# Attention phase of a fused attention and expert kernel: one hand-written order of six entries per block, queries and keys laid out by block

## Chip, cores and metric

One core of one Trainium2 chip. The metric is the device time of one execution in microseconds (us); the kernel before takes 626.17 us (median of 3 runs, 625.88 to 626.33).

## What is computed

Windowed attention over 2 batches, 8 heads, 576 positions and 64 columns a head; its output, 1152 tokens of 512 columns, goes through a dense mixture of 4 experts and then through a two-layer network. Everything is float32.

```python
scores = scale * np.matmul(q, k.transpose(0, 1, 3, 2))
mask = (rel >= 0) & (rel < 64)                    # rel = query position - key position
attn = softmax(np.where(mask, scores, -1e9))
x = attn @ v                                      # heads side by side: 1152 x 512
x = sum_e p[:, e] * (relu(x @ w1[e]) @ w2[e])     # 4 experts, 512 -> 1024 -> 512
h = x @ w_in                                      # 512 -> 2048
return (max(h, 0) + alpha * min(h, 0)) @ w_out    # 2048 -> 512
```

## The kernel before

Queries are taken in 18 blocks of 64 rows (9 to a batch); a block needs its own 64 keys and the 64 before it. Four pairs of heads are worked side by side, so that a block is 128 partitions (two heads of 64 queries) by 4 pairs by 128 keys. Every block j goes through these steps, each a function that issues instructions to several engines:

- **S** (`att_S`, L302): TensorE multiplies queries and keys (L309, 8 products, 16 records in the trace) into two PSUM banks; in the same function VectorE adds the mask and takes the row extreme, once for each pair (L320).
- **E** (`att_E`, L324): ScalarE takes the exponential with its row sum, once for each pair (L327).
- **N** (`att_N`, L330): VectorE adds 1e-9 and inverts the sums (L332, L333), GpSimd scales the block (L334).
- **PT** (`att_PT`, L336): TensorE transposes the four pairs (L340); ScalarE copies them out of PSUM (L346), or VectorE does (L344) for odd j from 4 on.
- **PV** (`att_PV`, L349): TensorE multiplies by the values (L357). The result is the token block x in three forms: raw (`xr`), a rounded high part and a low part. For the last block of a chunk ScalarE makes the high part (L365) and VectorE the low part (L366) and the copy (L367); else VectorE copies (L369) and GpSimd makes high and low (L370, L371). PV also loads the values of block j + 6.

The tokens are then taken in four chunks (256, 256, 256, 384). For the first slice of 512 expert columns, `l1_chunk` (called LC; **L c f**, L500) multiplies a chunk by 128 columns of w1 in 12 products of 256 columns, in the order w1-low by x-high, w1-high by x-low, w1-high by x-high; `l2_chunk` (BC; **B c t**, L533) multiplies by w2. The weights are split into high and low parts first: **W f** (`split_w1`, L228 ScalarE, L230 GpSimd for even f and VectorE for odd f) and **V f** (`split_w2`, L219 ScalarE, L212 VectorE). **X** (`x_second`) prepares sums for later slices, **R** (`p_prep`) the expert shares. After the fourth chunk come the other slices, over 500 us of products.

Order. The whole program runs under `manual_schedule`: an engine works through its instructions in the order in which the functions are called. That order is made by a loop over j that appends steps to a list (L603 on), and by marks: L 0 0 comes after PV 3 and four further steps, and after each L and B the list is advanced in proportion. The start is, as called:

```
S_0 E_0 S_1 E_1 N_0 S_2 E_2 N_1 W_0 PT_0 S_3 E_3 N_2 W_1 Q_3 PT_1 N_3 S_4 E_4 PV_0 W_2 PT_2 N_4
S_5 E_5 PV_1 W_3 PT_3 N_5 S_6 PV_2 Q_4 PV_3 E_6 PT_4 S_7 N_6 L_0_0 V_0 R L_0_1 V_1 E_7 PT_5 S_8 ...
```

The V splits are planned into L 0 0 to L 0 3. PSUM is eight banks taken in turn; S takes two, the others one.

Loads. All DMAs are issued by SyncE (SP) in program order: queries of a group of three blocks (`load_q`, L117, 384 KB; **Q g** later), keys (`load_k`, L120; first three blocks 384 KB, then the other six, 768 KB; batch 1 whole with Q 3), values (`load_v`, L129, L131), weight slices of 1 MB (`load_w`, L144, two buffers). A slice's load is placed after the last use of the slice two before it.

Of the kernel before, what the change touches and what calls it, by code (L numbers as in the profile page):

```python
# [8 lines left out]
F32 = mybir.dt.float32  # L9
# [7 lines left out]
P = 128  # L17
# [9 lines left out]
def tile_kernel(ctx, tc, q, k, v, probs, w1, w2, w_in, w_out, alpha, out):  # L27
    nc = tc.nc


    B, H, D, S = k.shape
    NP = H // 2
# [3 lines left out]
    BLK = 64  # L36
# [58 lines left out]
    for c in range(1, NCH):  # L95
        n = CHUNK[c + 1] - CHUNK[c]
        xc.append([w0.tile([P, KD, 384], F32R, tag=f"xc{w}", bufs=2, name=f"xc{w}{c}")[:, :, 0:n] for w in "hl"])
    kts = [ab.tile([P, NP, BLK + S], F32, name=f"kt{i}") for i in range(B)]

    qs = [ab.tile([P, NP, GRP], F32, name=f"q{i}") for i in range(3)]  # L100

# [12 lines left out]

    def load_q(g):
        b, i = divmod(g, S // GRP)
        nc.sync.dma_start(out=qs[g % 3], in_=q[b, i])  # L117

    def load_k(b, t0, t1):
        nc.sync.dma_start(out=kts[b][:, :, BLK + t0:BLK + t1],  # L120
                          in_=k[b].rearrange("(a h) d t -> (h d) a t", h=2)[:, :, t0:t1])

# [102 lines left out]
    def split_w1(f):  # L225
        hv, lv = [x.rearrange("p (k m) -> p k m", k=KD) for x in w_tiles(1, 0, f)]
        src = ws_t[1, 0][:, :, f * P:(f + 1) * P]
        nc.scalar.activation(out=hv, in_=src, func=AF.Copy)  # L228
        e = nc.vector if f % 2 else nc.gpsimd
        e.tensor_tensor(out=lv, in0=src, in1=hv.bitcast(F32), op=ALU.subtract)  # L230
# [65 lines left out]

    v_t, ws_t, wd_t, w_t, wf_t, h_t, p_t, pt_t = {}, {}, {}, {}, {}, {}, {}, {}

    def att_S(j):
        g, jb = divmod(j, GB)  # L300
        m = mask0 if j % NB == 0 else mask

        ps = [psum(f"s{j}_{i}")[:, 0:NP // 2 * P].rearrange("p (a k) -> p a k", k=P) for i in range(2)]
        sv = [ps[hp % 2][:, hp // 2, :] for hp in range(NP)]

        for hp in range(NP):
            for h in range(2):
# [40 lines left out]

    def att_PV(j):  # L349
# [230 lines left out]

    with tc.manual_schedule():
        load_q(0)
        load_k(0, 0, GRP)
        nc.vector.memset(kts[0][:, :, 0:BLK], 0.0)
        make_mask(mask0, True)
        load_v(0)
        load_v(1)
        make_identity(nc, ident)
        make_mask(mask, False)
        nc.gpsimd.memset(kts[1][:, :, 0:BLK], 0.0)  # L590
        load_k(0, GRP, S)
# [10 lines left out]

        NG = NBLK // GB  # L603
        steps = []
        for j in range(NBLK + 4):
            last = (j - 3) * BLK in CHUNK[1:]
            pv = [("PV", j - 4)] if 0 <= j - 4 < NBLK else []

            if last:
                steps += pv  # L610
            apart = 6 <= j - 1 < 14
            if apart:
                steps.append(("E", j - 1))
            if j == NBLK:
                steps.append(("N", j - 1))
            if 0 <= j - 3 < NBLK:
                steps.append(("PT", j - 3))
            if 3 < j < NBLK and not apart:
                steps.append(("N", j - 1))
            if j < NBLK:  # L620
                steps.append(("S", j))
                if not 6 <= j < 14:
                    steps.append(("E", j))
            if 0 < j <= 3:
                steps.append(("N", j - 1))
            if not last:
                steps += pv
            if apart:
                steps.append(("N", j - 1))
            if 2 <= j < 2 + NF:  # L630
                steps.append(("W", j - 2))
            if j % GB == 0 and 3 <= j // GB + 2 < NG:
                steps.append(("Q", j // GB + 2))

            if 12 <= j < 17:
                steps.append(("X", j - 12))
        pos = [0]

        def att_step():
            op, j = steps[pos[0]]  # L640
            pos[0] += 1
            if op == "Q":
                load_q(j)
                if j == 3:
                    load_k(1, 0, S)
            elif op == "S":
                att_S(j)
            elif op == "E":
                att_E(j)
            elif op == "N":  # L650
                att_N(j)
            elif op == "W":
                split_w1(j)
            elif op == "X":
# [23 lines left out]
        def LC(c):  # L678
            return [("LC", c, f) for f in range(NF)]
# [101 lines left out]

        marks = [steps.index(("PV", CHUNK[c + 1] // BLK - 1)) + 1 for c in range(NCH)]
        per = [len(LC(c) + BC(c)) for c in range(NCH)]
        while pos[0] < marks[0] + 4:
            att_step()
        for tid in loads.get(-1, ()):
# [9 lines left out]
        for i, unit in enumerate(order):  # L796
            op = unit[0]
            if op == "END":
                while pos[0] < len(steps):
                    att_step()  # L800
                at_cm.__exit__(None, None, None)
# [37 lines left out]
            if op in ("LC", "BC") and unit[1] < NCH - 1:  # L839
                c = unit[1]  # L840
                n = (unit[2] if op == "LC" else NF + unit[2]) + 1
                while pos[0] < min(len(steps), marks[c] + (marks[c + 1] - marks[c]) * n // (per[c] - 1)):
                    att_step()

# [38 lines left out]
```

## Time and profile before

| | |
|---|---|
| median of 3 runs | 626.17 us |
| profiled execution, its own time | 626.92 us |
| its span, first to last instruction | 624.9 us |
| PE busy | 610.9 us (98%) |
| ScalarE (ACT) busy | 316.6 us (51%) |
| VectorE (DVE) busy | 468.9 us (75%) |
| GpSimd (POOL) busy | 280.7 us (45%) |
| mean granted TensorE clock | 0.995 |

The sum of a change is made against the span. What lies around the span is 626.92 - 624.9 = 2.0 us. PE is TensorE's products, PEld its weight loads. A timeline row gives the start, the duration, engine, line, operation, what is written from what, and in brackets how long the engine sat idle before it and what released it.

### The profile page before, as it was taken

The page shows a single profiled execution, that of the slowest core. Times are in us where ns is not written, and L with a number is a line of the kernel's source. Part 1 is how long each engine was busy: PE and PEld are TensorE (multiplying, and loading weights), DVE is VectorE, ACT ScalarE, POOL GpSimd, SP SyncE. Part 2 cuts the span into 40 slices and gives each one's busy share as a digit, 9 for nine tenths or more (in the row PEclk, how much of TensorE's full clock was granted, in tenths as well). Part 3 has the DMA queues.
Part 4 walks back from the last instruction along what each step waited for, and adds up shares of the span by engine and source line. Part 5 has one row for each costly group of instructions (what it writes and reads, how often), then busy time and mean ns, then how long its engine had stood idle before and what let it go on. Part 6 is the DMA issues. An engine that isn't in the chain of part 4 may idle for free.

```text
span 624.9 us, 10887 instructions
## 1 busy us (share of the span) xinstructions
PE 610.9 (98%) x4032; PEld 549.2 (88%) x4032; DVE 468.9 (75%) x937; ACT 316.6 (51%) x789; POOL 280.7 (45%) x297
## 2 busy tenths in 40 slices
PE   4899999999999999999999999999999999999998
PEld 3688899989989989989989989988898988988986
DVE  3776659779888779878878879746978879764642
ACT  5656536634633724634633724635777753651730
POOL 5646661145153443445253443603735677661440
PEclk9799999999999999999999999999999999999999
DMA  9842002415414514415314514003401412310012
GB/s 320 314 160 65 6 1 65 139 34 177 161 51 144 160 35 151 153 59 180 135 50 141 164 34 131 39 7 120 145 1 36 157 79 69 105 64 1 2 50 102
DMA packets 31653, 62.60 MB, mean 100 GB/s; under 512 B 2288, under 2 KB 11760, under 8 KB 30576
## 3 DMA queue, kind: packets, MB, share of 16 engines
q1 hardware_dynamic: 31600, 61.90, 29.4%
q8 instruction: 32, 0.52, 0.3%
q14 instruction: 21, 0.17, 0.1%
HBM read 51.14 MB, written 10.75 MB: 99 GB/s over the span
## 4 chain that ended last, share of the span: by engine, by line
PE 96%; DMA 1%; ACT 1%; DVE 1%; SPq 0%; issue 0%
PE o L545 43%; PE X L431 23%; PE Z L431 11%; PE W L431 6%; PE h L500 5%; PE oc L533 4%; PE pv L357 1%; DMA ws<-in_moe_w_dram 1%; PE pt L340 1%; PE s L309 1%; ACT p L327 1%; PE x L578 1%; ACT w1h L228 0%; ACT ptr L346 0%; SPq L117 0%
## 5 line engine op out<-in xcount | busy, mean ns | idle before, releaser
L545 PE MATMUL o<-w2l,hh 128*128 128x512 f32 (+1 forms) x400 | 155.5, 389 | 0.0
L545 PE MATMUL o<-w2h,hl 128*128 128x512 f32 (+1 forms) x400 | 155.3, 388 | 0.0
L545 PE MATMUL o<-w2h,hh 128*128 128x512 f32 (+1 forms) x400 | 154.9, 387 | 0.0
L292 POOL TENSOR_TENSOR ct<-ct 128x512 f32<-128x512 f32 x32 | 44.0, 1374 | 118.8 <-DVE ct L291 53.3
L545 PEld LDWEIGHTS o<-w2h,hl 128*128 128x128 f32 x400 | 75.1, 188 | 16.5 <-POOL hl L526 1.2
L545 PEld LDWEIGHTS o<-w2h,hh 128*128 128x128 f32 x400 | 75.1, 188 | 14.8
L545 PEld LDWEIGHTS o<-w2l,hh 128*128 128x128 f32 x400 | 75.1, 188 | 14.5
L564 DVE SCALAR_TENSOR_TENSOR acc<-o,pn,acc 128x512 f32<-128x512 f32 x63 | 47.1, 748 | 38.8 <-PE o L545 38.6
L187 POOL TENSOR_TENSOR sr<-ws 128x256 f32<-128x256 f32 x44 | 40.7, 926 | 72.4 <-DVE wfl L212 61.5
L212 DVE SCALAR_TENSOR_TENSOR w2l<-ws,w2h 128x512 fp32r<-128x512 f32 x48 | 42.7, 896 | 20.8 <-ACT w2h L219 20.5
L431 PE MATMUL X<-xth,wfl 128*128 128x256 f32 (+1 forms) x264 | 56.7, 296 | 0.0
L431 PE MATMUL X<-xtl,wfh 128*128 128x256 f32 (+1 forms) x264 | 56.6, 295 | 0.0
L431 PE MATMUL X<-xth,wfh 128*128 128x256 f32 (+1 forms) x264 | 56.6, 295 | 0.0
L219 ACT ACTIVATE wfh<-sr 128x1024 fp32r<-128x1024 f32 x22 | 23.2, 1058 | 53.5 <-POOL sr L187 53.5
L293 POOL TENSOR_TENSOR ct<-ct 128x512 f32<-128x512 f32 x32 | 47.3, 1478 | 2.5
L280 ACT ACTIVATE ct<-wd 128x512 f32<-128x512 f32 x32 | 21.3, 667 | 47.4 <-DVE ct L286 47.4
L568 DVE TENSOR_TENSOR acc<-o,acc 128x512 f32<-128x512 f32 (+1 forms) x28 | 18.8, 670 | 33.2 <-PE o L545 33.1
L431 PEld LDWEIGHTS X<-xtl,wfh 128*128 128x128 f32 x264 | 42.7, 190 | 0.0
L431 PEld LDWEIGHTS X<-xth,wfl 128*128 128x128 f32 x264 | 42.7, 190 | 0.0
L431 PEld LDWEIGHTS X<-xth,wfh 128*128 128x128 f32 x264 | 42.6, 190 | 0.0
L526 POOL TENSOR_TENSOR hl<-s,hh 128x256 fp32r<-128x256 f32 (+1 forms) x16 | 13.3, 852 | 61.2 <-ACT hh L525 61.2
L431 PE MATMUL Z<-xth,wfl 128*128 128x320 f32 (+1 forms) x176 | 37.9, 296 | 0.0
(155 smaller groups left out, 1425.9 us busy)
## 6 DMA issues: line engine op xcount, KB each, us to landing
ws<-in_moe_w_dram SPq DMA_DIRECT2D x16, 1024.0 KB, 5.6
wd<-in_moe_w_in_dram SPq DMA_DIRECT2D x16, 512.0 KB, 3.8
cv<-ct SPq DMA_DIRECT2D x32, 256.0 KB, 2.7
wd<-in_moe_w_out_dram SPq DMA_DIRECT2D x16, 512.0 KB, 3.6
ws<-cv SPq DMA_DIRECT2D x8, 1024.0 KB, 5.3
v<-in_v_dram SPq DMA_DIRECT2D x16, 256.0 KB, 5.2
q<-in_q_dram SPq DMA_DIRECT2D x6, 384.0 KB, 6.6
out_dram<-acc SPq DMA_DIRECT2D x8, 256.0 KB, 2.0
```

What stands on the lines that cost most here:

```text
L187: e.tensor_tensor(out=t4[:, o], in0=x, in1=y, op=op)
L212: nc.vector.scalar_tensor_tensor(out=lv, in0=src, scalar=1.0, in1=hv.bitcast(F32), op0=ALU.mult, op1=ALU.subtract)
L219: nc.scalar.activation(out=hv, in_=src, func=AF.Copy)
L280: nc.scalar.activation(out=a, in_=top.bitcast(F32), func=AF.Abs, scale=LIFT)
L292: nc.gpsimd.tensor_tensor(out=y, in0=y, in1=e, op=ALU.mult)
L293: nc.gpsimd.tensor_tensor(out=y, in0=r, in1=y, op=ALU.add)
L431: nc.tensor.matmul(ps, lhsT=w[:, d, :], rhs=x[:, d, :], start=(first and m == 0), stop=(m == 5), skip_group_check=True)
L500: nc.tensor.matmul(ps, lhsT=w[:, d * P:(d + 1) * P], rhs=x[:, d, :], start=(m == 0), stop=(m == 3 * KD - 1))
L533: nc.tensor.matmul(ps, lhsT=h_c[c, f][a][:, t * P:(t + 1) * P], rhs=w_t[2, 0, f][b], start=(n == 0), stop=(n == 3 * NF - 1))
L545: nc.tensor.matmul(ps, lhsT=h_t[s, p, f][a][:, t * P:(t + 1) * P], rhs=w_t[2, s, f][b][:, cols], start=(n == 0), stop=(n == 3 * NF - 1))
L564: nc.vector.scalar_tensor_tensor(out=at, in0=ps, scalar=sc, in1=at, op0=ALU.mult, op1=ALU.add)
L568: nc.vector.tensor_tensor(out=at, in0=ps, in1=at, op=ALU.add)
```

## The change

- `att_S` is cut in two: **S** keeps the products, the masking becomes **M** (`att_M`). Blocks have six entries: S, M, E, N, PT, PV.
- The loop and the marks go. One table names every step of the attention phase, with W, V, R, Q, X and the places of L and B.
- Queries lie in DRAM and SBUF as (block, pair, 64), keys too, with one empty block in front. The products take the keys of two neighbouring blocks as two pieces of 64. The first block of queries and of keys is loaded by DMAs of its own (128 KB each), the other two blocks of the group after them. The later keys of both batches come in two parts; the order of the first loads is another.
- PT 0 and PT 1 are copied by VectorE. PV 2 is handled like the last block of a chunk. W's low part goes to VectorE for even f, to GpSimd for odd f.
- The load of w1's next slice stands after L 0 0 in program order, ahead of W 3.

```diff
-    kts = [ab.tile([P, NP, BLK + S], F32, name=f"kt{i}") for i in range(B)]
-    qs = [ab.tile([P, NP, GRP], F32, name=f"q{i}") for i in range(3)]
+    kts = [ab.tile([P, NB + 1, NP, BLK], F32, name=f"kt{i}") for i in range(B)]
+    qs = [ab.tile([P, GB, NP, BLK], F32, name=f"q{i}") for i in range(3)]
...
+    def load_q(g, a=0, z=GB):
         b, i = divmod(g, S // GRP)
-        nc.sync.dma_start(out=qs[g % 3], in_=q[b, i])
+        nc.sync.dma_start(out=qs[g % 3][:, a:z], in_=q[b, i, :, a:z])
+    def load_k(b, a, z):
+        nc.sync.dma_start(out=kts[b][:, 1 + a:1 + z], in_=k[b, :, a:z])
...
-        e = nc.vector if f % 2 else nc.gpsimd
+        e = nc.gpsimd if f % 2 else nc.vector
...
                 nc.tensor.matmul(
-                    sv[hp][c],
-                    lhsT=qs[g % 3][r, hp, jb * BLK:(jb + 1) * BLK],
-                    rhs=kts[j // NB][r, hp, (j % NB) * BLK:(j % NB) * BLK + P],
+                    sv[hp][c].rearrange("p (n t) -> p n t", n=2),
+                    lhsT=qs[g % 3][r, jb, hp, :],
+                    rhs=kts[j // NB][r, j % NB:j % NB + 2, hp, :],
...
+        m_t[j] = sv, m
+    def att_M(j):
+        sv, m = m_t.pop(j)
...
-        if j % 2 and j >= NF:
+        if j in (0, 1) or j % 2 and j >= NF:
             nc.vector.tensor_copy(out=t, in_=src)
...
-        if (j + 1) * BLK in CHUNK:
+        if j == 2 or (j + 1) * BLK in CHUNK:
...
+        load_q(0, 0, 1)
+        load_k(0, 0, 1)
+        nc.vector.memset(kts[0][:, 0], 0.0)
         make_mask(mask0, True)
+        load_q(0, 1, GB)
+        load_k(0, 1, GB)
         load_v(0)
...
         load_q(1)
+        load_k(0, GB, 2 * GB)
+        load_v(1)
         load_w((1, 0))
         load_v(2)
         load_v(3)
+        load_k(0, 2 * GB, NB)
+        load_q(2)
         load_w((2, 0))
         load_v(4)
         load_v(5)
...
-                if j == 3:
-                    load_k(1, 0, S)
+                if j in (3, 4):
+                    load_k(1, *((0, GB) if j == 3 else (GB, NB)))
...
+        TABLE = (
+            "S_0 S_1 M_0 M_1 E_0 N_0 S_2 M_2 S_3 Q_3 E_1 N_1 M_3 PT_0 E_2 N_2 E_3 S_4 M_4 N_3 PT_1 S_5 PV_0 "
+            "E_4 M_5 PT_2 PV_1 N_4 W_0 PT_3 PV_2 W_1 PV_3 S_6 Q_4 W_2 E_5 M_6 N_5 S_7 L_0_0 V_0 W_3 E_6 M_7 "
+            "S_8 N_6 M_8 V_1 L_0_1 PT_4 L_0_2 V_2 L_0_3 V_3 E_7 PT_5 PV_4 N_7 E_8 S_9 Q_5 S_10 PT_6 M_9 R_0 "
+            "N_8 B_0_0 E_9 M_10 PV_5 E_10 PV_6 PT_7 B_0_1 PV_7 PT_8 S_11 N_9 M_11 L_1_0 N_10 E_11 L_1_1 PT_9 "
...
+            "M_16 L_2_2 E_16 PV_12 X_4 PT_14 N_16 S_17 L_2_3 M_17 E_17 PV_13 N_17 PT_15 B_2_0 PV_14 PT_16 "
+            "PV_15 PT_17 PV_16 PV_17 B_2_1")
...
-        tids = [(1, 0)] + tids
-        uses[1, 0] = [-1]
+        tids = [(1, 0), (2, 0)] + tids
+        uses[1, 0], uses[2, 0] = [last_use["W"]], [last_use["V"]]
```

## Rows read from the trace of the kernel before

**Rows 1.** Busy time by stretch: us, then PE, PEld, DVE, ACT, POOL (instructions), granted clock, DMA share, GB/s

```profile
5.73:14.87 9.14, 7.05 (x89) 5.33 (x89) 5.07 (x38) 7.14 (x33) 3.46 (x4) 1.00 1.05 385
14.87:22.35 7.48, 4.52 (x92) 3.35 (x88) 4.75 (x24) 6.54 (x24) 6.19 (x8) 0.96 1.06 384
22.35:25.52 3.17, 3.17 (x37) 2.39 (x37) 2.86 (x14) 2.00 (x10) 2.62 (x4) 0.50 1.06 373
25.52:29.85 4.33, 4.33 (x29) 4.33 (x26) 2.08 (x14) 1.31 (x3) 1.83 (x3) 0.64 0.80 262
...
29.85:84.16 54.31, 54.14 (x630) 45.44 (x629) 36.44 (x153) 29.78 (x116) 32.36 (x41) 1.00 0.21 67
84.16:624.90 540.74, 537.67 (x3169) 488.33 (x3167) 417.40 (x695) 268.56 (x604) 230.64 (x224) 1.00 0.27 91
```

**Rows 2.** The same view for one pair of first-layer units, L 1 0 and L 1 1

```profile
45.53:48.51 2.98, 2.98 (x28) 2.98 (x25) 1.62 (x11) 0.55 (x2) 1.04 (x1) 1.00 0.05 14
```

**Rows 3.** Timeline of TensorE

```profile
5.73 2.83 PE L309 MATMUL s<-kt,q 64*64 64x128 f32 x48 [5.73 <-DMA kt<-in_k_dram]
10.65 1.11 PE L340 MATMUL pt<-ident,p 128*128 128x128 f32 x4 [2.09 <-POOL p L334]
...
13.81 1.13 PE L309 MATMUL s<-kt,q 64*64 64x128 f32 x16
14.87 0.71 PE L357 MATMUL pv<-ptr,v 128*64 128x64 f32 x16
...
16.44 0.67 PE L309 MATMUL s<-kt,q 64*64 64x128 f32 x16
...
22.35 1.12 PE L357 MATMUL pv<-ptr,v 128*64 128x64 f32 x16 [2.03 <-ACT ptr L346]
...
25.52 1.22 PE L500 MATMUL h<-xah,w1l 128*128 128x256 f32 x4
```

**Rows 4.** Timeline of ScalarE

```profile
7.34 0.40 ACT L327 ACTIVATE p<-sm,st 128x128 f32<-128x128 f32 x1 [5.33 <-DVE st L320]
...
8.90 0.39 ACT L327 ACTIVATE p<-sm,st 128x128 f32<-128x128 f32 x1
...
21.21 0.61 ACT L228 ACTIVATE w1h<-ws 128x512 fp32r<-128x512 f32 x1
21.73 0.57 ACT L346 ACTIVATE ptr<-pt 128x512 f32<-128x512 f32 x1
...
23.52 0.39 ACT L365 ACTIVATE xah<-pv 128x256 fp32r<-128x256 f32 x1 [1.22 <-PE pv L357]
```

**Rows 5.** Timeline of VectorE, the first two masking instructions of block 0

```profile
7.01 0.29 DVE L320 CUSTOM_DVE_ANT_0 sm<-s,mask 128x128 f32<-128x128 f32 x1 [5.88 <-PE s L309]
...
7.22 0.29 DVE L320 CUSTOM_DVE_ANT_0 sm<-s,mask 128x128 f32<-128x128 f32 x1
```

**Rows 6.** Groups of instructions, 0 to 25.5 us: count, busy us, mean ns, idle before

```profile
L334 POOL TENSOR_TENSOR p<-p,st 128x512 f32<-128x512 f32 x6 | 6.2, 1038 | 7.0 <-DVE st L333 6.6 <-PE pv L357 0.4
L332 DVE TENSOR_SCALAR st<-st 128x4 f32<-128x4 f32 x6 | 2.5, 417 | 1.3 <-ACT p L327 1.3
L230 POOL TENSOR_TENSOR w1l<-ws,w1h 128x512 fp32r<-128x512 f32 x2 | 2.5, 1270 | 1.1 <-ACT w1h L228 1.0
L230 DVE TENSOR_TENSOR w1l<-ws,w1h 128x512 fp32r<-128x512 f32 x2 | 1.4, 692 | 2.0 <-ACT w1h L228 2.0
```

**Rows 7.** First two windows of 5 us, last two columns DMA share and GB/s

```profile
0.00:5.00 5.00, 0.00 (x0) 0.00 (x0) 0.27 (x1) 1.28 (x1) 3.63 (x17) 1.00 0.63 197
5.00:10.00 5.00, 2.83 (x48) 2.46 (x48) 2.72 (x25) 2.66 (x14) 0.44 (x1) 1.00 1.05 369
...
```

**Rows 8.** DMA issue to landing, first query transfer, first key transfer, first weight slice

```profile
q<-in_q_dram SPq DMA_DIRECT2D x1, 384.0 KB, 3.0
...
kt<-in_k_dram SPq DMA_DIRECT2D x1, 384.0 KB, 4.4
...
ws<-in_moe_w_dram SPq DMA_DIRECT2D x1, 1024.0 KB, 8.6
```

More of the change, by code (lines that the diff above doesn't have):

```diff
@@ L28, in tile_kernel @@
     nc = tc.nc
-    B, H, D, S = k.shape
+    B, S, H, D = v.shape
     NP = H // 2
@@ L112, in make_mask @@
             nc.gpsimd.memset(m[:, 0:BLK], NEG)
-    def load_q(g):
+    def load_q(g, a=0, z=GB):
         b, i = divmod(g, S // GRP)
-        nc.sync.dma_start(out=qs[g % 3], in_=q[b, i])
-    def load_k(b, t0, t1):
-        nc.sync.dma_start(out=kts[b][:, :, BLK + t0:BLK + t1],
-                          in_=k[b].rearrange("(a h) d t -> (h d) a t", h=2)[:, :, t0:t1])
+        nc.sync.dma_start(out=qs[g % 3][:, a:z], in_=q[b, i, :, a:z])
+    def load_k(b, a, z):
+        nc.sync.dma_start(out=kts[b][:, 1 + a:1 + z], in_=k[b, :, a:z])
     def load_v(j):
@@ L295, in conv_steps @@
         store()
-    v_t, ws_t, wd_t, w_t, wf_t, h_t, p_t, pt_t = {}, {}, {}, {}, {}, {}, {}, {}
+    v_t, ws_t, wd_t, w_t, wf_t, h_t, m_t, p_t, pt_t = {}, {}, {}, {}, {}, {}, {}, {}, {}
     def att_S(j):
@@ L581, in tile_kernel @@
     with tc.manual_schedule():
-        load_q(0)
-        load_k(0, 0, GRP)
-        nc.vector.memset(kts[0][:, :, 0:BLK], 0.0)
+        load_q(0, 0, 1)
+        load_k(0, 0, 1)
+        nc.vector.memset(kts[0][:, 0], 0.0)
         make_mask(mask0, True)
+        load_q(0, 1, GB)
+        load_k(0, 1, GB)
         load_v(0)
-        load_v(1)
         make_identity(nc, ident)
         make_mask(mask, False)
-        nc.gpsimd.memset(kts[1][:, :, 0:BLK], 0.0)
-        load_k(0, GRP, S)
+        nc.gpsimd.memset(kts[1][:, 0], 0.0)
         load_q(1)
+        load_k(0, GB, 2 * GB)
+        load_v(1)
         load_w((1, 0))
@@ L595, in tile_kernel @@
         load_v(3)
+        load_k(0, 2 * GB, NB)
+        load_q(2)
         load_w((2, 0))
-        load_q(2)
         load_v(4)
@@ L601, in tile_kernel, with att_step @@
         nc.sync.dma_start(out=alph, in_=alpha)
[L603 to L641, printed above, removed]
+        def att_step(op, j):
             if op == "Q":
                 load_q(j)
-                if j == 3:
-                    load_k(1, 0, S)
+                if j in (3, 4):
+                    load_k(1, *((0, GB) if j == 3 else (GB, NB)))
             elif op == "S":
                 att_S(j)
+            elif op == "M":
+                att_M(j)
             elif op == "E":
@@ L653, in att_step @@
                 split_w1(j)
+            elif op == "V":
+                split_w2(0, j)
+            elif op == "R":
+                p_prep()
             elif op == "X":
@@ L682, in BC @@
             return [("BC", c, t) for t in range((CHUNK[c + 1] - CHUNK[c]) // P)]
-        order = LC(0) + BC(0) + LC(1) + BC(1) + LC(2) + BC(2) + [("END",)]
-        order += LC(3) + [("X1",)] + BC(3)
+        TABLE = (
[8 rows of a table added]
+        order, steps, last_use = [], [[]], {}
+        for word in TABLE.split():
+            op, *j = word.split("_")
+            j = [int(x) for x in j]
+            if op in ("L", "B"):
+                order.append((op + "C", *j))
+                steps.append([])
+            else:
+                steps[-1].append((op, *j))
+                last_use[op] = len(order) - 1
+        order += [("END",)] + LC(3) + [("X1",)] + BC(3)
         for s in range(1, S1):
@@ L698, in plan @@
             work.setdefault(at[unit], []).append((fn, tid, args))
-        for f in range(NF):
-            plan(("LC", 0, f), split_w2, (2, 0), 0, f)
         for s in range(1, NST):
@@ L780, in tile_kernel @@
                 loads.setdefault(free, []).append(tid)
[L782 to L785, printed above, removed]
+        for step in steps[0]:
+            att_step(*step)
         for tid in loads.get(-1, ()):
@@ L798, in tile_kernel @@
             if op == "END":
-                while pos[0] < len(steps):
-                    att_step()
                 at_cm.__exit__(None, None, None)
@@ L814, in tile_kernel @@
             elif op == "LC":
-                while pos[0] < marks[unit[1]]:
-                    att_step()
                 l1_chunk(*unit[1:])
@@ L824, in tile_kernel @@
                     pend.append((i + 2, unit[2], unit[3]))
-            if i == 0:
-                p_prep()
             while pend and pend[0][0] <= i:
@@ L839, in tile_kernel @@
             if op in ("LC", "BC") and unit[1] < NCH - 1:
[L840 to L843, printed above, removed]
+                for step in steps[i + 1]:
+                    att_step(*step)
 _INS = ['q', 'k', 'v', 'moe_domain_probs', 'moe_w1', 'moe_w2', 'moe2_w_in', 'moe2_w_out', 'moe2_alpha']
@@ L862 @@
             b, h, s, d = a.shape
-            a = _np.ascontiguousarray(a.reshape(b, h // 2, 2, s // 192, 192, d).transpose(0, 3, 2, 5, 1, 4).reshape(b, s // 192, 2 * d, h // 2, 192))
+            a = a.reshape(b, h // 2, 2, s // 192, 3, 64, d).transpose(0, 3, 2, 6, 4, 1, 5)
+            a = _np.ascontiguousarray(a.reshape(b, s // 192, 2 * d, 3, h // 2, 64))
         elif name == "k":
-            a = _np.ascontiguousarray(a.transpose(0, 1, 3, 2))
+            b, h, s, d = a.shape
+            a = a.reshape(b, h // 2, 2, s // 64, 64, d).transpose(0, 2, 5, 3, 1, 4)
+            a = _np.ascontiguousarray(a.reshape(b, 2 * d, s // 64, h // 2, 64))
         elif name == "v":
```

2 rows, old and new, of the table TABLE are left out of this document.

## The prediction, made before the change was run

> **What bounds the kernel now.** I read the busy table by stretch first [rows 1]. From 29.85 us on TensorE is busy 54.14 of 54.31 us and then 537.67 of 540.74, so nothing that moves work among the other engines is worth anything there; the reader should see that the loss lies ahead of 29.85. It has three parts. Until 5.73 us TensorE waits for keys [rows 3]. From 5.73 to 22.35 it works 7.05 + 4.52 of 16.6 us. From 22.35 to about 28.6 it works without pause at the 1.2 GHz level (granted clock 0.50, then 0.64 on the mean of the next 4.33 us) [rows 1].
>
> The timelines say why. TensorE comes to PV 3 at 22.35 after 2.03 us of waiting for ScalarE's copy of PT 3 [rows 3]; on ScalarE that copy starts at 21.73, right behind W 3 at 21.21 [rows 4]. ScalarE is busy 7.14 of 9.14 us, then 6.54 of 7.48 [rows 1]: it is the bound there, and in its order stand things that the first L does not need yet. Up to that copy it does six E (1.56 us each, from 7.34 to 8.90 [rows 4]), four W and four copies (0.52 and about 0.55 each [rows 4]): 9.4 + 2.1 + 2.2 = 13.7 of the 15 us since 7.34. L 0 0 starts at 25.52 [rows 3].
>
> The clock needs a word. The record says 1.00 from the start, but an S takes 1.13 us at 13.81 and 0.67 at 16.44, and PV at 14.87 is the first fast step [rows 3]; I go by the durations: 1.2 GHz until 14.87, 2.4 until about 21.8, 1.2 again after the wait of 2.03 us. A step (S, PT, PV) costs some 1.05 us at the low level and 0.6 at the high one, from start to start.
>
> **The change, part by part.** I walk the new order from the first landing to L 0 0; all times below are estimates put together from the rows named.
>
> First landing. Before, 384 KB of queries landed at 0.73 + 3.0 = 3.7 us and the keys at 1.17 + 4.4 = 5.57 [rows 8]. Now S 0 needs 256 KB in two transfers. Bounds: 3.2 (128 KB less than the queries) and 5.57 (no gain); I take 3.7, the nearest row. S 1 and S 2 need the same 768 KB as before: 5.5. The second group ends with byte 1.70 MB: 0.985 MB are moved by 5.0 us (197 GB/s), the rest at 369 GB/s takes 1.95 [rows 7], and some 0.95 passes to landing: S 3 at 8.0. W1's slice comes 0.39 MB earlier in the queue than before, where it landed at 3.87 + 8.6 = 12.4 [rows 8], so at about 11.4; ScalarE asks for it at 15.5. Two more DMA issues cost SP about 0.45 us each, hidden since the engines are full until 25 us [rows 1]. The 384 KB of later keys and queries that now stand ahead of w2 put it at about 17.5; V 0 asks at 20.
>
> Masks and exponentials. M starts 1.28 us after its S (5.73 to 7.01) and takes 4 x 0.21 = 0.85 [rows 5]; E starts 0.33 after M [rows 4, 5]. N takes 0.42 + 0.18 on VectorE and 1.04 on GpSimd [rows 6]. So M 0 5.0, E 0 5.3 to 6.9, M 1 6.8 to 7.65, E 1 7.1 to 8.7, N 0 7.65 to 8.25, GpSimd 8.35 to 9.4. M 2 8.25, E 2 8.7 to 10.25, M 3 9.7 (behind N 1), E 3 10.25 to 11.8.
>
> TensorE, low clock: PT 0 9.4, S 4 10.45, PT 1 11.5, S 5 12.55, PV 0 13.6. VectorE copies PT 0 at 10.55 to 11.2 (0.69, like its W part [rows 6]), N 2 to 11.8, M 4 to 12.65, N 3 to 13.25, copy of PT 1 to 13.95. E 4 12.15 to 13.7. TensorE is then dense from 9.4 on. Before, the first step at the high level was a PV that ended a dense run of PT and S [rows 3]; so I take the high level from PV 0 on. PV 0 ends 14.3, PT 2 14.9, PV 1 15.5, PT 3 16.1.
>
> ScalarE: copy of PT 2 14.95 to 15.5, W 0 to 16.05, copy of PT 3 16.1 to 16.65, high part of PV 2 16.85 to 17.2 (0.39 [rows 4]), W 1 to 17.75, high part of PV 3 to 18.1. VectorE: raw copy of PV 0 to 14.7, M 5 to 15.55, copy of PV 1 to 16.0, N 4 to 16.6, W 0's low part (0.69) to 17.3, PV 2's to 18.1, PV 3's low part to 18.55. GpSimd holds W 1's low part (1.27 [rows 6]) until about 19.5; L 0 1 asks at 20.8. TensorE: PV 2 16.1, PV 3 16.8, S 6 and S 7 17.45 to 18.65. **L 0 0 starts at about 18.6**; its low x parts are asked 0.47 later.
>
> Sum. L 0 0 comes 25.52 - 18.6 = 6.9 us earlier. It and L 0 1 run at the high clock: before they took 4.33 us [rows 1], another pair takes 2.98 [rows 2], 1.35 gained. PT 4 stood ahead of L 0 0 and now stands behind: 0.6 back. Gain 6.9 + 1.35 - 0.6 = 7.7 us. Bounds: if ScalarE had no gap from 5.3 on, five E, two copies, two W and two high parts take 7.8 + 1.1 + 1.1 + 0.7 = 10.7 and L 0 0 starts at 16.1, a gain of 10.2. Below, the rivals.
>
> A rule on the clock. The row shows TensorE rising to the high level at 14.87 out of a run in which PT and S took turns [rows 3]. The Trainium skill, TensorE: Matmul & The Clock Gate, Part 4: PE-mode transpose, says that transposes do not bring up the full clock, as they don't count as busy like other products. By that rule the new stretch, with its four PT, would stay low, and the gain would be 2.9 instead of 7.7. The sum goes by the row.
>
> Moves that cost nothing, and their cover. E 5, W 2, W 3 and R go behind or close to L 0 0: ScalarE's 3.1 us and VectorE's share then run beside four L (6 us) and S 8 to S 10; in the stretch after, ScalarE was busy 29.78 and VectorE 36.44 of 54.31 [rows 1]. W 3's low part on GpSimd ends at about 23, L 0 3 asks at 24.5; without that 1.5 us TensorE would stand. The load of w1's next slice now waits on SP for W 3's low part; behind it stand values of blocks 10 and up, first read 20 us later. M 9 on VectorE waits behind N 7, which waits for E 7 until 28.6; PT 7 asks for N 7 near 33. The thinnest cover is at L 1 0: between PV 7 and it stand now only PT 8 and S 11 (1.2 us), for a high part of 0.39 and a low one of 0.4; before, B 0 1 (3 us) stood there. If ScalarE is late there, up to 1 us is lost.
>
> Keys in two pieces of 64. No row streams an operand in two pieces. Below: no gain, the columns are as many. Above: each S like two runs of 64-column products, PV's 0.71 [rows 3], so 1.42 instead of 0.67. I take 0: as many instructions and elements.
>
> From L 0 0 on TensorE has no idle time to lose or save [rows 1], so the gain stays to the end: span 624.9 - 7.7 = 617.2, and with the 2.0 us around it 619.2 for a profiled execution. The profiled 626.92 lies 0.75 above the median, so I take 626.17 - 7.7 = **618.5**.
>
> **Rivals.**
> - Half clock. TensorE stays at 1.2 GHz until after L 0 0: twelve steps from 9.4 on (PT 0 to S 7) x 1.05 = 12.6, L 0 0 at 22.0, the 1.35 not gained. Gain 25.5 - 22.0 - 0.6 = 2.9: 623.3. For: the low level came back before after 2 us of idling. Against: the rise at 14.87. This is what the rule above would do. 0.08.
> - Gaps behind L 0 0. ScalarE, late with E 5 to E 8, or the thin cover at L 1 0, opens three gaps of 0.8 us: 2.4 lost, 620.9. For: ScalarE's queue holds about 11 us of work in the 10 after L 0 0. Against: the covers above. 0.14.
> - No early landing. The small transfers share the engines with those behind them, and S 0 starts at 5.5: the chain moves by up to 1.8, gain 5.9, 620.3. 0.08.
> - Slower. The two-piece keys cost each S 0.75 more (1.42 for 0.67): four S in the dense run before L 0 0 and ten behind it, 14 x 0.75 = 10.5, net 2.8 lost, 629.0. It is slower from 0.64 us more per S on (14 x 0.64 is the 7.7 gained and 1.25 beyond). Against: TensorE's time goes by columns streamed. 0.05.
>
> **Chances.** 0.65 for the forecast with its own range of 616.0 to 620.2. The range for all, 616.0 to 622.2, takes in the gaps and the late landing and leaves out the half clock, the slower case and a little at the ends, some 0.18. About 0.2% (1.25 us) is what a measurement of this kernel can tell from no change. Faster by more: all but the slower case and its milder forms, 0.93; within: 0.02; slower: 0.05.
>
> **What would show it.** Right: the first S near 3.7 and the first L near 18.6 us; granted clock 1.00 from there on; a pair of L at 3.0 us; the stretch from L 0 0 to the fourth chunk 57 to 58 us with TensorE without gaps; S steps of 0.67. Wrong: clock 0.50 around L 0 0; idle TensorE rows ahead of L 1 0 or PT 7, released by ScalarE or GpSimd; S steps over 0.8; the first S still at 5.5.

## The result, and the profile after

| | before | changed |
|---|---|---|
| median | 626.02 us (4 runs, 625.80 to 626.33) | **620.38 us** (4 runs, 619.03 to 620.71) |
| profiled execution | 626.92 us | 620.26 us |
| its span | 624.9 us | 618.2 us |

The ratio is 0.9904, with a 95% interval of 0.9888 to 0.9919: 0.96% faster, 5.64 us where 7.67 were forecast. The time of 618.5 was 1.9 us too low: 620.38 is inside the range for all (616.0 to 622.2), but 0.2 us above the forecast's own range of 616.0 to 620.2.

The busy table by stretch shows where the gain lies. The cuts are the first S, S 3, the first step at the high clock level, L 0 0, the fourth chunk and the end; columns as in [rows 1].

```profile
3.91:9.21 5.30, 3.11 (x48) 2.37 (x49) 2.78 (x25) 3.20 (x16) 1.19 (x4) 1.00 0.95 312
9.21:14.49 5.28, 5.28 (x56) 3.63 (x57) 4.39 (x26) 4.74 (x26) 3.14 (x4) 1.00 1.05 399
14.49:19.30 4.81, 4.74 (x108) 3.89 (x105) 3.82 (x17) 3.48 (x9) 3.95 (x6) 1.00 1.05 378
19.30:77.32 58.02, 57.60 (x660) 48.57 (x657) 43.67 (x178) 34.72 (x137) 38.10 (x47) 1.00 0.38 129
77.32:618.20 540.88, 537.67 (x3169) 488.33 (x3167) 417.55 (x695) 268.59 (x604) 231.48 (x224) 1.00 0.27 91
```

Read from the end. The last stretch took 540.74 us [rows 1] and takes 540.88. The one before it, from L 0 0 on, took 84.16 - 25.52 = 58.64 and takes 58.02. So 6.2 of the 6.7 us of span are gained before L 0 0, and the rest is the first two L at full speed, less one PT that moved behind them and 0.25 us of waiting shown below. From S 3 to PV 0 (the second row) TensorE is the bound: 5.28 busy of 5.28 us, with ScalarE busy 4.74. Before, in the stretch from the first fast step to PV 3, ScalarE was the fuller one, 6.54 of 7.48 us against 4.52 [rows 1].

TensorE's timeline of the changed kernel, columns as in [rows 3]:

```profile
3.91 1.13 PE L308 MATMUL s<-kt,q 64*64 64x128 f32 x16 [3.91 <-DMA kt<-in_k_dram]
6.07 1.98 PE L308 MATMUL s<-kt,q 64*64 64x128 f32 x32 [1.03 <-DMA kt<-in_k_dram]
9.21 1.13 PE L308 MATMUL s<-kt,q 64*64 64x128 f32 x16 [1.17 <-DMA kt<-in_k_dram]
10.28 1.11 PE L343 MATMUL pt<-ident,p 128*128 128x128 f32 x4
...
13.43 1.13 PE L308 MATMUL s<-kt,q 64*64 64x128 f32 x16
14.49 0.69 PE L360 MATMUL pv<-ptr,v 128*64 128x64 f32 x16
...
16.89 1.44 PE L360 MATMUL pv<-ptr,v 128*64 128x64 f32 x32
18.27 1.10 PE L308 MATMUL s<-kt,q 64*64 64x128 f32 x32
19.30 0.74 PE L503 MATMUL h<-xah,w1l 128*128 128x256 f32 x4
...
20.92 0.67 PE L308 MATMUL s<-kt,q 64*64 64x128 f32 x16
...
25.34 0.74 PE L503 MATMUL h<-xah,w1l 128*128 128x256 f32 x4 [0.25 <-POOL w1l L229]
```

These are the forecast's steps: S 0 comes at 3.91 (3.7 was forecast), S 1 at 6.07 (5.5), S 3 at 9.21 (8.0), PV 0, the first fast step, at 14.49 (13.6), and L 0 0 at **19.30** (18.6). PV 2 and PV 3 stand at 16.89 as one row of 32: the wait of 2.03 us ahead of PV 3 [rows 3] is gone. The first third of L 0 0 takes 0.74 us and not 1.22 [rows 3]. From there to L 0 3 TensorE idles once, 0.25 us. An S at the high level takes 0.67, as before [rows 3], with its keys in two pieces. Each of the three early idle rows waits for a landing of keys.

ScalarE's timeline of the changed kernel, some of its rows:

```profile
5.52 0.40 ACT L330 ACTIVATE p<-sm,st 128x128 f32<-128x128 f32 x1 [3.51 <-DVE st L323]
...
7.66 0.40 ACT L330 ACTIVATE p<-sm,st 128x128 f32<-128x128 f32 x1 [0.49 <-DVE st L323]
...
12.93 0.40 ACT L330 ACTIVATE p<-sm,st 128x128 f32<-128x128 f32 x1 [0.54 <-DVE st L323]
...
15.80 0.60 ACT L349 ACTIVATE ptr<-pt 128x512 f32<-128x512 f32 x1 [1.22 <-PE pt L343]
...
17.00 0.60 ACT L349 ACTIVATE ptr<-pt 128x512 f32<-128x512 f32 x1
17.63 0.39 ACT L368 ACTIVATE xah<-pv 128x256 fp32r<-128x256 f32 x1
```

The copy of PT 3 starts at 17.00 instead of 21.73 [rows 4], and between E 0 and L 0 0 ScalarE now waits for others three times, 2.25 us in all, while TensorE has no idle row from S 3 to L 0 0. ScalarE is no longer what sets L 0 0.

### The profile page after: what moved, and what is told of

It reads as the page before. It is cut to its first block, busy times and chain, and to the rows that moved or that the text cites. A ratio compares the mean times of both kernels' runs of the same rounds, so it can differ in the third digit from the quotient of the medians.

```text
span 618.2 us, 10887 instructions
## 1 busy us (share of the span) xinstructions
PE 608.4 (98%) x4032; PEld 546.8 (88%) x4032; DVE 472.5 (76%) x940; ACT 316.0 (51%) x788; POOL 280.8 (45%) x295
## 4 chain that ended last, share of the span: by engine, by line
PE 97%; DMA 1%; SPq 0%; POOL 0%; ACT 0%; DVE 0%; issue 0%
PE o L548 44%; PE X L434 23%; PE Z L434 11%; PE W L434 6%; PE oc L536 4%; PE h L503 4%; PE pt L343 2%; PE pv L360 2%; PE s L308 2%; DMA kt<-in_k_dram 1%; PE x L581 1%; POOL w1l L229 0%; SPq L117 0%; POOL p L337 0%; SPq L120 0%
```

## The experiments

After the result I held this: the gain is the order on ScalarE; the layout and the early landing give nothing by themselves; and the changed kernel's first stretch is bound by TensorE at the 1.2 GHz level behind a late S 3. The rivals were that the loads bring part of the gain, and that ScalarE's chain of exponentials is still the bound. Medians and ratios below are against the kernel before on the same chip (medians 626.1 to 626.2 us); "first L" is the start of L 0 0 in the profiled execution.

**1. The old order with the new layout and loads.** S and masking are one step again, and engine assignments as well as the loop and marks are those of before.

```diff
-        if j in (0, 1) or j % 2 and j >= NF:
+        if j % 2 and j >= NF:
...
-        if j == 2 or (j + 1) * BLK in CHUNK:
+        if (j + 1) * BLK in CHUNK:
...
-        for step in steps[0]:
-            att_step(*step)
+        marks = [steps.index(("PV", CHUNK[c + 1] // BLK - 1)) + 1 for c in range(NCH)]
+        per = [len(LC(c) + BC(c)) for c in range(NCH)]
+        while pos[0] < marks[0] + 4:
+            att_step()
```

> Kernel: the order of before with the new layout and the new loads (first block's landing alone). The changed kernel stands at 620.4 us, the kernel before at 626.0. Theory A (the hand-written order makes the gain; ScalarE's queue ahead of PV 3 was the bound): the earlier landing starts ScalarE's first E near 5.5 instead of 7.3 us, but E 1 waits for the second landing; ScalarE's chain and with it the first L come 0.5 to 1.8 us earlier, 624.2 to 625.5, and the granted clock still drops near 22 us. Theory B (the early landing makes the gain): 621.5 or less. Theory C (loads and layout do nothing for the old order): 626.0.

Measured: 626.33 us (10 runs, 625.47 to 628.39), ratio 0.9999 (0.9984 to 1.0013). TensorE's timeline of this kernel:

```profile
3.45 1.13 PE L308 MATMUL s<-kt,q 64*64 64x128 f32 x16 [3.45 <-DMA kt<-in_k_dram]
...
22.30 0.69 PE L356 MATMUL pv<-ptr,v 128*64 128x64 f32 x16 [1.84 <-ACT ptr L345]
...
25.05 0.74 PE L499 MATMUL h<-xah,w1l 128*128 128x256 f32 x4 [0.88 <-POOL xah L369]
```

S 0 comes 2.3 us earlier than before, and PV 3 comes at 22.30 against 22.35 [rows 3], again behind ScalarE. Under the old order, the layout and the loads give nothing. One more thing shows on ScalarE, in its timeline:

```profile
12.41 0.63 ACT L227 ACTIVATE w1h<-ws 128x512 fp32r<-128x512 f32 x1 [2.24 <-DMA ws<-in_moe_w_dram]
```

W 0, which the old order puts ahead of the copy of PT 0, waits 2.24 us for w1's slice: an earlier start met a landing that had not moved with it.

**2. ScalarE's order put back in one place.** E 5, W 2 and W 3 stand ahead of the copy of PT 3 again; all else is the changed kernel.

```diff
-            "... PV_1 N_4 W_0 PT_3 PV_2 W_1 PV_3 S_6 Q_4 W_2 E_5 M_6 N_5 S_7 L_0_0 V_0 W_3 E_6 M_7 "
+            "... PV_1 N_4 W_0 E_5 W_2 W_3 PT_3 PV_2 W_1 PV_3 S_6 Q_4 M_6 N_5 S_7 L_0_0 V_0 E_6 M_7 "
```

> Kernel: the changed one with E 5, W 2 and W 3 put back ahead of the copy of PT 3 on ScalarE, as in the order of before; all else as changed. Theory A (what stands ahead of that copy on ScalarE was the bound before): 1.56 + 2 x 0.53 = 2.6 us more ahead of the copy, PV 3 waits that much with TensorE idle, the first L comes 2.0 to 2.6 us later, and if the clock falls in that wait, 1 to 3 us more: 622.4 to 626.0. Rival (ScalarE has slack there, the gain comes from elsewhere): within 0.5 us of 620.4.

Measured: 623.46 us (7 runs, 622.48 to 624.85), ratio 0.9952 (0.9936 to 0.9968). TensorE's timeline:

```profile
20.12 0.69 PE L360 MATMUL pv<-ptr,v 128*64 128x64 f32 x16 [2.44 <-ACT ptr L349]
...
22.32 1.22 PE L503 MATMUL h<-xah,w1l 128*128 128x256 f32 x4
```

And one row of 1 us of its busy table:

```profile
22.00:23.00 1.00, 1.00 (x11) 0.68 (x4) 0.97 (x11) 0.00 (x0) 0.91 (x2) 0.50 1.03 365
```

The three steps bring back both losses of the kernel before: the wait of PV 3 (2.44 us, 2.03 in [rows 3]) and then the low clock level under the first L (0.50 granted, 1.22 us for its first third as in [rows 3]). They cost 2.4 to 3.1 us against the two medians of the changed kernel (620.38, and 621.02 in experiment 4), about half of the gain. This shows that what stands ahead of that copy on ScalarE was the largest cause, the wait and the clock together.

**3. The first landing whole.** Queries and keys of the first three blocks come in one transfer each, as before.

```diff
-        load_q(0, 0, 1)
-        load_k(0, 0, 1)
+        load_q(0)
+        load_k(0, 0, GB)
...
-        load_q(0, 1, GB)
-        load_k(0, 1, GB)
```

> Kernel: the changed one, but queries and keys of the first three blocks land whole again (two DMAs of 384 KB). Theory D, the prediction's walk (the chain from the first S over ScalarE's E sets the first L): S 0 comes 1.7 us later, the first L some 1.5 us later, 621.6 to 622.3. Theory E (from S 3 on TensorE itself, dense at the 1.2 GHz level, sets the first L; S 3 waits for the second group's keys at 9.2 us, which land no later here): E 0 to E 3 have slack, the first L stays near 19.3 and the time within 0.4 us of 620.4.

Measured: 619.22 us (4 runs, 618.53 to 620.25), ratio 0.9885 (0.9860 to 0.9909). It is not slower; its median is 1.2 us below the changed kernel's, and the intervals overlap. TensorE's timeline:

```profile
5.16 2.84 PE L308 MATMUL s<-kt,q 64*64 64x128 f32 x48 [5.16 <-DMA kt<-in_k_dram]
8.31 1.03 PE L308 MATMUL s<-kt,q 64*64 64x128 f32 x16 [0.31 <-DMA kt<-in_k_dram]
10.09 0.66 PE L343 MATMUL pt<-ident,p 128*128 128x128 f32 x4 [0.75 <-POOL p L337]
...
17.76 0.74 PE L503 MATMUL h<-xah,w1l 128*128 128x256 f32 x4
```

S 0 is 1.25 us later than in the changed kernel and S 3 is 0.9 earlier; then the clock is up at PT 0 (0.66 against 1.11), and L 0 0 comes 1.5 us earlier. Part of the reason for S 3 is in the issues. The same key transfer for S 3 in SyncE's timeline, first in this kernel:

```profile
2.85 0.43 SPq L120 DMA_DIRECT2D kt<-in_k_dram  x1
```

and in the changed one, where two more issues stand ahead of it:

```profile
1.65 0.42 SPq L117 DMA_DIRECT2D q<-in_q_dram  x1
2.11 0.43 SPq L120 DMA_DIRECT2D kt<-in_k_dram  x1
...
3.80 0.43 SPq L120 DMA_DIRECT2D kt<-in_k_dram  x1
```

0.95 us later at issue, 0.90 later at S 3. That is the smallest delay on record: in the five other traces with the new order, these first loads and no idle products (experiments 2, 4 and 8) the same transfer is issued at 3.78 to 3.80, too, and S 3 comes at 9.52 to 10.31. So beyond the issues up to 1 us more passes before the keys land. The transfers did not make it up: the DMA view of 4.5 to 6 us gives, for the changed kernel,

```profile
DMA packets 160, 0.30 MB, mean 201 GB/s; under 512 B 29, under 2 KB 29, under 8 KB 160
```

and for the whole landing

```profile
DMA packets 175, 0.44 MB, mean 296 GB/s; under 512 B 19, under 2 KB 19, under 8 KB 175
```

The same kernel was run again beside later ones.

> Kernel: the one with the whole first landing once more, for its spread. Theory J (the two DMAs saved let everything behind them land 0.8 us earlier, S 3 at 8.3 instead of 9.2 to 10.0 us, and ScalarE runs without a gap from E 0 to W 2): 618.5 to 620.3 again, below the changed kernel's 619.9 to 621.2 of the last job, ratio to before 0.987 to 0.990. Rival (the first run's lead was the luck of the clock): 620.4 to 621.0, ratio 0.991 to 0.992.

Measured: 618.52 us (4 runs, 618.35 to 619.79), ratio 0.9885 (0.9868 to 0.9901), first L at 17.79. Both runs together: the split of the first landing brings nothing and costs 1.2 to 2.5 us against the two medians of the changed kernel (the second follows).

**4. The changed kernel again**, unaltered, as a measure of its spread.

> Kernel: the changed one once more, unaltered, for the spread of its executions. Theory F (the execution's time hangs on when TensorE's granted level goes up in the first 15 us; where a profile shows it up before PT 0 the first L starts near 17.8 us, where it is up at PV 0 near 19.3): times spread over some 1.5 us, 618.9 to 620.7, and in this profile the first L and the rise go together. Rival (the spread has another source): the first L stays at 19.3 whatever the clock does.

Measured: 621.02 us (5 runs, 619.93 to 621.23), ratio 0.9914 (0.9901 to 0.9928), S 3 at 9.99, first L at 19.63. The first fast step was S 5, in TensorE's timeline:

```profile
14.20 0.69 PE L308 MATMUL s<-kt,q 64*64 64x128 f32 x16
```

Differences to the changed kernel of under 0.6 us mean nothing below.

**5. The clock raised by idle products.** TensorE multiplies the empty block in front of the keys with itself, ahead of S 0 and behind S 0 and S 2, where it would wait.

```diff
+        def warm(n):
+            for i in range(8 * n):
+                r = slice(D * (i % 2), D * (i % 2) + D)
+                nc.tensor.matmul(
+                    wt[r, 0:P].rearrange("p (n t) -> p n t", n=2),
+                    lhsT=kts[0][r, 0, 0, :],
+                    rhs=kts[0][r, 0, 0:2, :],
...
+        warm(2)
...
+                if j in (0, 2):
+                    warm(1)
```

> Kernel: the changed one with extra products of zeros on TensorE, two S-like steps of 8 ahead of S 0 and one each in the gaps behind S 0 and S 2; their results are not used. Theory E (the dense run at 1.2 GHz from S 3 to S 5 is the bound): the high level comes before S 3, the six steps from 9.2 to 14.5 us take 0.6 instead of 1.05 each, then ScalarE and VectorE bind, and the first L comes near 17.4 instead of 19.3: 618.0 to 619.0. Theory D (ScalarE's chain binds whatever the clock): within 0.4 us of 620.4. If the extra products delay S 0 or S 1, up to 0.5 us slower.

Measured: 618.55 us (4 runs, 618.28 to 620.42), ratio 0.9882 (0.9852 to 0.9912). One of the four took 620.42, and the interval overlaps the changed kernel's, so the reading rests on the trace. TensorE's timeline:

```profile
9.64 0.78 PE L308 MATMUL s<-kt,q 64*64 64x128 f32 x16 [1.82 <-DMA kt<-in_k_dram]
...
17.82 0.74 PE L503 MATMUL h<-xah,w1l 128*128 128x256 f32 x4
```

S 3 is even later than in the changed kernel (9.64 against 9.21), yet L 0 0 comes 1.5 us earlier: from S 3 to L 0 0 it is 8.2 us instead of 10.1. In the changed kernel it was TensorE's own speed that set this stretch, not ScalarE.

**6. S 3's landing, two ways.** First, on top of experiment 5, queries and keys of block 3 land alone too: two more DMAs.

```diff
+        load_q(1, 0, 1)
+        load_k(0, GB, GB + 1)
...
-        load_q(1)
-        load_k(0, GB, 2 * GB)
+        load_q(1, 1, GB)
+        load_k(0, GB + 1, 2 * GB)
```

> Kernel: the one with the extra products of zeros, and the second group's first block of queries and keys lands in DMAs of its own ahead of the first values, so that S 3 no longer waits (1.82 us of idle TensorE in the run with the extra products alone). Theory G (with the clock up, S 3's landing is the next bound: VectorE idles 1.00 and ScalarE 0.23 us for it): M 3 starts near 9.4 instead of 10.3, the first L near 17.0 instead of 17.8, 617.2 to 618.0. Rival (VectorE's and ScalarE's queues behind it, W and the parts of PV 2 and PV 3, absorb it): 618.3 to 618.7.

Measured: 619.66 us (5 runs, 618.37 to 621.48), ratio 0.9898 (0.9881 to 0.9914), first L at 18.75. S 3 no longer waits, but in TensorE's timeline the wait has moved to S 6:

```profile
17.71 1.10 PE L308 MATMUL s<-kt,q 64*64 64x128 f32 x32 [1.27 <-DMA q<-in_q_dram]
```

This split, too, paid for one early block with a later one. So, second, no DMA more: on top of experiment 5 the first values are loaded behind S 3's keys.

```diff
-        load_v(0)
...
         load_q(1)
         load_k(0, GB, 2 * GB)
+        load_v(0)
         load_v(1)
```

> Kernel: split first landing with the extra products of zeros, and the first values (128 KB) behind the second group's queries and keys. S 3 lands 0.3 to 0.4 us earlier than with the extra products alone (9.64); ScalarE's gap of 0.23 us ahead of E 3 goes: 618.0 to 618.6. Rival (ScalarE and VectorE are full behind it): 618.5 to 619.

Measured: **618.38 us** (4 runs, 618.27 to 618.47), ratio 0.9876 (0.9862 to 0.9891). TensorE's timeline:

```profile
8.60 0.78 PE L308 MATMUL s<-kt,q 64*64 64x128 f32 x16
10.03 0.66 PE L343 MATMUL pt<-ident,p 128*128 128x128 f32 x4 [0.64 <-POOL p L337]
...
17.58 0.74 PE L503 MATMUL h<-xah,w1l 128*128 128x256 f32 x4
```

S 3 does not wait, and from here on it is the exponentials: ScalarE has no idle row between E 0 (6.23) and 16 us, and PT 0 waits for GpSimd's scaling. This is the lowest median, 2.0 us under the changed kernel, with the smallest spread of all runs. Its lead over the whole landing (618.52, 619.22) is inside the spread.

**7. Whole landing and idle products together.**

```diff
+        load_q(0)
+        load_k(0, 0, GB)
...
+        warm(3)
...
+                if j == 2:
+                    warm(1)
```

> Kernel: whole first landing, and extra products of zeros on TensorE: three S-like steps ahead of S 0 and one behind S 2. Theory E with J: clock up before S 0, no gap on ScalarE from E 0 at 6.3 on, the first L near 17.3, 617.6 to 618.6, with a smaller spread than the whole landing alone. Rival (clock up or not, ScalarE's chain from E 0 at 6.8 on binds): as the whole landing alone.

Measured: 619.10 us (4 runs, 618.12 to 619.90), ratio 0.9887 (0.9872 to 0.9902); the profiled execution is the slowest of the four. No gain over the whole landing alone. TensorE's timeline:

```profile
10.15 0.66 PE L343 MATMUL pt<-ident,p 128*128 128x128 f32 x4 [1.49 <-POOL p L337]
...
11.68 0.97 PE L343 MATMUL pt<-ident,p 128*128 128x128 f32 x4 [0.28 <-POOL p L337]
```

and one row of 1 us of the busy table:

```profile
12.00:13.00 1.00, 1.00 (x12) 0.67 (x14) 1.00 (x9) 1.00 (x6) 0.71 (x1) 0.50 1.06 420
```

Here the level was up early and fell again, after an idle row of 1.49 us and a second of 0.28; it stayed at 0.50 until 15 us, and L 0 0 came at 19.15.

**8. The three smaller reassignments, each put back alone.** The copies of PT 0 and PT 1 on ScalarE:

```diff
-        if j in (0, 1) or j % 2 and j >= NF:
+        if j % 2 and j >= NF:
```

> Kernel: the changed one with the copies of PT 0 and PT 1 on ScalarE, as before. Theory H (ScalarE's queue ahead of PV 3 was what the change relieved): 2 x 0.5 us more there, of which its idle time in the changed profile (0.54 and 1.22 us ahead of E 4 and of the copy of PT 2) hides part: 0.2 to 1.0 us slower, 620.4 to 621.4. Rival (VectorE is the bound of the new order): 1.2 us come off VectorE, 619.0 to 619.8.

Measured: 621.32 us (4 runs, 620.89 to 622.06), ratio 0.9923 (0.9909 to 0.9936). ScalarE's timeline:

```profile
12.52 0.60 ACT L349 ACTIVATE ptr<-pt 128x512 f32<-128x512 f32 x1 [3.31 <-PE pt L343]
```

E 2 stands behind that copy, and ScalarE waits 3.31 us for PT 0 with exponentials it could do. Some 1.1 us of that are a late landing in this execution (S 3 at 10.31, 9.21 in the changed kernel's trace). The price is 0.3 to 0.9 us against the two medians of the changed kernel; the lower figure is inside the spread, so the time alone does not show it.

W's low parts as before, even ones on GpSimd:

```diff
-        e = nc.gpsimd if f % 2 else nc.vector
+        e = nc.vector if f % 2 else nc.gpsimd
```

> Kernel: the changed one with the low parts of W as before, W 0 and W 2 on GpSimd, W 1 and W 3 on VectorE. GpSimd's 1.27 us for W 0 stands behind the parts of PV 0 and PV 1 and ends near 19.7, the first L needs it: 0.3 to 1.0 us slower, 620.5 to 621.3; TensorE's wait of 0.25 us ahead of L 0 3 for W 3 goes. Rival (no matter who does W): within 0.3 us of 620.2.

Measured: 621.91 us (4 runs, 621.75 to 622.07), ratio 0.9931 (0.9917 to 0.9945). TensorE's timeline:

```profile
21.65 0.74 PE L503 MATMUL h<-xah,w1l 128*128 128x256 f32 x4 [1.48 <-POOL w1l L229]
```

GpSimd's timeline has the cause, W 0's low part, which starts behind PV's parts and a scaling:

```profile
19.88 1.72 POOL L229 TENSOR_TENSOR w1l<-ws,w1h 128x512 fp32r<-128x512 f32 x1
```

0.9 to 1.5 us, on the path.

PV 2 handled like any other block:

```diff
-        if j == 2 or (j + 1) * BLK in CHUNK:
+        if (j + 1) * BLK in CHUNK:
```

> Kernel: the changed one with PV 2 handled as before: VectorE copies, GpSimd makes high and low part. GpSimd then works PV 1's and PV 2's parts, N 4 and W 1's low part one behind the other, PV 2's low part is ready near 20.5 where the first L asks for it at 19.8, and W 1's low part near 21.8 where L 0 1 asks at 21.5: 0.4 to 1.2 us slower, 620.8 to 621.8. Rival (the 0.3 us off ScalarE and 0.35 us off VectorE count more): 619.8 to 620.4.

Measured: 620.93 us (4 runs, 620.10 to 621.98), ratio 0.9918 (0.9903 to 0.9933). TensorE's timeline:

```profile
20.17 0.73 PE L503 MATMUL h<-xah,w1l 128*128 128x256 f32 x4 [0.46 <-POOL xah L373]
...
21.31 0.74 PE L503 MATMUL h<-xal,w1h 128*128 128x256 f32 x4 [0.40 <-POOL xal L374]
```

The trace shows 0.86 us lost there, the medians 0 to 0.55: too little to be called shown by the time. The single prices, 2.4 to 3.1, 0.9 to 1.5, 0.3 to 0.9 and 0 to 0.5 us, add up to 3.6 to 6.0, and the whole gain is 5.2 to 5.6; but single prices need not add, and the last two are not clear of the spread. What order and assignments are worth as a whole stands in experiment 1: with the same layout and loads 626.33 against 620.38 and 621.02, so 5.3 to 6.0 us. The order accounts for the gain, and the split landing adds nothing to it. The new order on the old layout was not run.

## Why the prediction was right and where it was wrong

**Right: the place and the cause.** That there was nothing to gain behind the first two L was read from [rows 1], and the stretches behind them confirm it. That ScalarE's order made the wait, and the wait the low clock, was read from [rows 3, 4]; experiment 2 makes both appear again. The clock does not follow the wait every time: in experiment 1 PV 3 waits 1.84 us and L 0 0 still runs at full speed.

**Right: the run to L 0 0.** From PV 0 to L 0 0 the forecast had 5.0 us and the chip took 4.81. The dense run from PT 0 came, with the rise of the level at its end. The rule in the Trainium skill, TensorE: Matmul & The Clock Gate, Part 4: PE-mode transpose, spoke against that rise; it came at 14.49 out of S and PT in turn, as in [rows 3]. Either the S in such a run are enough or the rule does not hold here; no run had transposes alone.

**Wrong: the first landing.** The step was "Two more DMA issues cost SP about 0.45 us each, hidden since the engines are full until 25 us", with S 3 at 8.0. The two issues did cost 0.47 each, and were not hidden: S 3's keys were issued 0.95 later than with a whole landing, and S 3 came at 9.21. I took the engines as full from [rows 1], which begin at 5.73 us; in the first 5 us, when these issues were made, their share was 0.63 [rows 7]. And the rate itself changed with the transfers: the row of 5 to 10 us read 369 GB/s before [rows 7], and reads 321 in the changed kernel and 265 in experiment 4. 1.2 us of delay at S 3 became 0.9 at PV 0 and 0.7 at L 0 0. I had the mechanism among the rivals ("the small transfers share the engines with those behind them", 620.3), but bound it to a late S 0. That its 620.3 is nearly the measured time is luck: with S 0 at 5.16 the kernel of experiment 3 was not slower. S 0 was early, as forecast, and worth nothing, as TensorE then waited at S 1 and S 3.

**Wrong: what starts the dense run.** The walk had PT 0 at 9.4, released by GpSimd's scaling of block 0, with S 3 done before it and TensorE dense from there. In the changed kernel that scaling, in GpSimd's timeline, is

```profile
8.71 1.04 POOL L337 TENSOR_TENSOR p<-p,st 128x512 f32<-128x512 f32 x1 [3.98 <-DVE st L336]
```

and ends at about 9.75; PT 0 starts at 10.28, behind S 3 and without a wait. These 0.88 us are the delay at PV 0. The upper bound of the gain was made for ScalarE without gaps. In the changed kernel it has gaps of 0.49, 0.54 and 1.22 us, and TensorE at the low level, behind S 3, has none. Experiment 5 shows which of the two set the stretch: same order, S 3 later, first L 1.5 us earlier.

**Wrong: from one execution to the median.** The gain was summed against a profiled execution and then taken off the median, 0.75 us below it. But part of the sum, the 1.35 us of the first L pair at the low level, is not in every execution. Of 32 later executions of the kernel before, 9 show a mean granted clock of 0.999 or more and average 625.8 us, and 23 show 0.992 to 0.997 and average 626.6; the profiled one had 0.995 and took 626.92, 0.3 above the average of its group. So the 0.75 us are in part the low level, which most executions share, and in part something else in that execution that no run set apart. Experiment 1, the old order, was profiled at 0.999 with a first third of L of 0.74 us. The changed kernel's profiled execution lies at its own median (620.26, 620.38). So the 1.88 us of error are 1.0 of span (618.2 for 617.2, of which 0.7 lie ahead of L 0 0) and 0.9 of this conversion. The forecast for a profiled execution, 619.2, was 1.1 too low.

**The covers.** W 3's low part was forecast for about 23 and ended at 25.3; it cost the 0.25 us seen ahead of L 0 3. That is all that was lost there; the stretch took 58.02 for the 57.9 that follow from the sum. No idle row stands ahead of L 1 0 or PT 7, and the moved load of w1's next slice cost nothing that shows.

**The rivals.** Half clock: no, L at 0.74 with a granted clock of 1.00. Gaps behind L 0 0: 0.25 and not 2.4 us. Slower by two-piece keys: no, S at 0.67.

## What to carry to other kernels

On an engine that works in order, what stands ahead of the instruction that others wait for can cost nearly its full time (in experiment 2 three steps, a wait of 2.44 us), and the clock as well; sort by who asks first. A first transfer cut in two brought its own block forward here and put what stood behind it on the queue back, by 0.95 us at issue and more at landing: look for the next wait before paying for it. Before a gain summed on one profiled execution is taken off a median, find out whether the loss that goes away is in every execution.

## What the runs showed of the hardware that was not expected

- The clock record reads 1.00 in the first stretches (9.21 to 14.49 above) while an S takes 1.13 us, and the same S takes 0.67 later: the level there is read from durations.
- When the level rises differs between executions of the same kernel: the changed kernel's first fast step was PV 0 at 14.49 with S 3 at 9.21, and in experiment 4 S 5 at 14.20 with S 3 at 9.99. What stands ahead counts, too. In the whole landing S 3 followed the first three S after 0.31 us, and the level was up at PT 0 (10.09); in the kernel before 2.09 us of idle followed them [rows 3], and it rose at 14.87. First L's at 17.6 to 17.8 go with an early rise (experiments 3, 5 and the second of 6), 19.2 to 19.6 with a rise at about 14.3 or a fall in between. The whole landing's two groups of times (618.4 to 618.6, and 619.8 to 620.3) may be this; its two traces are both of the fast group, so it stays open.
- The fall differs, too: the level was low after PV 3's wait of 2.03 us [rows 3] and after the 2.44 of experiment 2, and stayed up after the 1.84 of experiment 1.
- W's low part took 0.69 us on VectorE and 1.27 on GpSimd [rows 6]. In the changed kernel the same instructions took 0.78 and 1.75 on VectorE and 1.29 and 1.75 on GpSimd. The two long ones start while the other engine is at work on another low part, of W or of V. W 1's on GpSimd and W 2's on VectorE, in their timelines:

```profile
19.42 1.29 POOL L229 TENSOR_TENSOR w1l<-ws,w1h 128x512 fp32r<-128x512 f32 x1
19.51 1.75 DVE L229 TENSOR_TENSOR w1l<-ws,w1h 128x512 fp32r<-128x512 f32 x1
```

  And V 0's on VectorE and W 3's on GpSimd:

```profile
22.62 1.51 DVE L211 SCALAR_TENSOR_TENSOR w2l<-ws,w2h 128x512 fp32r<-128x512 f32 x1
...
23.54 1.75 POOL L229 TENSOR_TENSOR w1l<-ws,w1h 128x512 fp32r<-128x512 f32 x1
```

  The one that starts second is the long one, and so it is in the other traces where two such parts overlap by 0.5 us or more: W's low part takes 1.74 to 1.76 us on VectorE in four traces, each time 0.1 us behind one on GpSimd, and the 1.72 us on GpSimd in the second part of experiment 8 begin 0.36 us behind one on VectorE. So W 2's long part holds up N 5 on VectorE, and W 3's low part, which GpSimd takes behind N 5's scaling, comes late. No run takes one of the two away alone, so what in the engines does this stays open.
